# Four token blocks deferred to a last phase that uses Strassen's seven products for both feed-forward matrix products

## The chip, the cores and the metric

The kernel runs on one core of a Trainium2 chip. The metric is the time of one execution on the device in microseconds (us). The core has a matrix engine (TensorE; PE in the profile, with PEld for its weight loads), VectorE (DVE), ScalarE (ACT), GpSimd (POOL) and a queue engine (SyncE, SP) that issues the transfers here. Each engine takes its instructions strictly in program order and waits for the others through semaphores.

## What is computed

Block-causal attention over 8 batches, 8 heads, 576 positions and head width 64, and then a feed-forward network on the 4608 tokens of width 512, with hidden width 2048:

```python
def _attn_ref(q, k, v):                     # (8, 8, 576, 64) each
    scores = scale * np.matmul(q, k.transpose(0, 1, 3, 2))
    scores = np.where(block_i >= block_j, scores, -1000000000.0)   # blocks of 64 positions
    scores = scores - np.max(scores, axis=-1, keepdims=True)
    attn = np.exp(scores)
    attn = attn / (np.sum(attn, axis=-1, keepdims=True) + 1e-09)
    return np.matmul(attn, v)

def _moe_ref(x, w_in, w_out):               # x: (4608, 512), from all heads of a token
    h = x @ w_in                            # (512, 2048)
    g = h * (1.0 / (1.0 + np.exp(-h)))      # silu
    return g @ w_out                        # (2048, 512)
```

## The kernel before

All matrix products are done in a rounded 32-bit form. To keep the precision, each operand is split into a high part (a rounded copy, by ScalarE: `hi`, `x_hi`, `g_hi`, `p_hi`, `split_hi`) and a low part (the rest, by GpSimd: `lo`, `x_lo`, `g_lo`, `p_lo`, `split_lo`). A product is then three matmuls: high by high, high by low, low by high.

**Attention** has 64 units, one for each batch and head (`Unit`). A unit's steps are: `scores` (TensorE, into three banks of the accumulation memory, named S), `max` and `max2` (VectorE), `sub` (VectorE: scores minus maximum into T, which frees the banks), `exp` and `p_hi` (ScalarE), `p_lo` (GpSimd), `sums` (VectorE), `pv` (TensorE, into U), `lower` (ScalarE), `fold` (VectorE, into the feature tile xu), and for each second head `mult` by the reciprocal sums and then `x_hi` and `x_lo`, which put the features of two heads into the ring `xbuf` of 16 tiles. The first positions of each batch are done apart (`First`, `Second`).

**The feed-forward part** has 18 blocks of 256 tokens with 8 steps each. A step is four pieces on TensorE, called "ffn" in the code: twice `ffn1` (12 matmuls of 256 columns each into h) and twice `ffn2` (6 matmuls of 512 columns each into o, two steps later), with `silu` and `g_hi` on ScalarE and `g_lo` on GpSimd between them. A ring tile is free when the last step of its block has read it.

**The order** of all engines' work is the program's order. A written-out list, ORDER, gives it for the weights' preparation and the first 17 units. A loop then takes each further unit i in a fixed order: scores and max of i, fold and mult of i-2, max2 of i, the split of i+1, some pieces (`ffn(pace - 3)`), the features of i-2, sums and pv of i-1, sub of i, lower of i-1, exp, p_hi and p_lo of i, and `ffn(3)`. What is left of the pieces is run behind the loop. The pace is set by one line:

```python
pace = 6 + (count[0] <= AHEAD + 7 * (i - TABLE))
```

## Time and profile before

| What | Value |
|---|---|
| Median of 3 runs | 1041.24 us (1041.07 to 1041.69) |
| Profiled execution, span | 1040.4 us |
| TensorE busy | 1032.7 us, 99% |
| VectorE, ScalarE, GpSimd busy | 762.8, 745.9 and 750.0 us |
| Moved by transfers | 79.95 MB |
| Attention's last score group starts | at 889.45 us |

The time of the profiled execution itself is not recorded apart from its span; the runs' median lies 0.84 us above the span. In the timeline a row has the start, the time to the end of the row's last instruction, the engine, the source line, the output and the input by their names in the program, and how many instructions of the kind follow one another. A duration of a matmul row holds the time until its result has left the array, so the cost of a group on TensorE is the distance to the start of the next group. In brackets is how long the engine was idle before the row, and who ended it.

### The profile page before, as it was taken

The page shows a single profiled execution, that of the slowest core. Times are in us where ns is not written, and L with a number is a line of the kernel's source. Part 1 is how long each engine was busy: PE and PEld are TensorE (multiplying, and loading weights), DVE is VectorE, ACT ScalarE, POOL GpSimd, SP SyncE. Part 2 cuts the span into 40 slices and gives each one's busy share as a digit, 9 for nine tenths or more (in the row PEclk, how much of TensorE's full clock was granted, in tenths as well). Part 3 has the DMA queues.
Part 4 walks back from the last instruction along what each step waited for, and adds up shares of the span by engine and source line. Part 5 has one row for each costly group of instructions (what it writes and reads, how often), then busy time and mean ns, then how long its engine had stood idle before and what let it go on. Part 6 is the DMA issues. An engine that isn't in the chain of part 4 may idle for free.

```text
span 1040.4 us, 20218 instructions
## 1 busy us (share of the span) xinstructions
PE 1032.7 (99%) x7162; PEld 938.7 (90%) x7162; DVE 762.8 (73%) x2233; ACT 745.9 (72%) x1192; POOL 750.0 (72%) x726
## 2 busy tenths in 40 slices
PE   8999999999999999999999999999999999999998
PEld 8888899999999999999999999998999999989987
DVE  7998499999968988888878888888888888700000
ACT  4876498888987888787878787878787777722222
POOL 5775679988997878787878787878787878622221
PEclk9999999999999999999999999999999999999999
DMA  7865232232222222232222222222222222000000
GB/s 264 280 212 198 75 97 74 71 87 67 65 71 74 54 55 74 54 81 59 82 56 75 59 75 54 65 64 54 75 55 74 55 74 55 25 3 21 1 21 21
DMA packets 35188, 79.95 MB, mean 77 GB/s; under 512 B 4752, under 2 KB 13200, under 8 KB 35088
## 3 DMA queue, kind: packets, MB, share of 16 engines
q1 hardware_dynamic: 35088, 78.66, 27.2%
q8 instruction: 57, 0.93, 0.4%
q14 instruction: 43, 0.35, 0.1%
HBM read 69.21 MB, written 9.44 MB: 76 GB/s over the span
## 4 chain that ended last, share of the span: by engine, by line
PE 89%; POOL 4%; DVE 3%; DMA 1%; issue 1%; ACT 1%; SPq 0%; POOLq 0%; DVEq 0%; ACTq 0%
PE h L620 36%; PE o L660 36%; PE S L308 8%; PE U L387 8%; POOL pl L363 1%; DMA qk<-in_qk_dram 1%; PE S L660 1%; DVE wm L235 1%; PE S L578 1%; POOL qh L284 1%; DMA wst<-in_moe_w_out_dram 1%; POOL g L638 1%; DVE S L229 0%; POOL ql L286 0%; DVE S L225 0%
## 5 line engine op out<-in xcount | busy, mean ns | idle before, releaser
L620 PE MATMUL h<-x,wi 128*128 128x256 f32 x3456 | 441.0, 282 | 0.3 <-POOL x L424 0.3
L620 PEld LDWEIGHTS h<-x,wi 128*128 128x128 f32 x3456 | 430.0, 188 | 11.5 <-issue 0.5
L660 PE MATMUL o<-wo,g 128*128 128x512 f32 (+1 forms) x1680 | 423.9, 397 | 0.0
L660 PEld LDWEIGHTS o<-wo,g 128*128 128x128 f32 x1680 | 305.7, 188 | 62.6 <-issue 0.7
L363 POOL TENSOR_TENSOR pl<-p,ph 128x448 fp32r<-128x448 f32 (+1 forms) x192 | 226.0, 1202 | 92.9 <-ACT ph L355 92.9
L638 POOL TENSOR_TENSOR g<-g,g 128x512 fp32r<-128x512 f32 x144 | 186.4, 1294 | 120.3 <-ACT g L633 110.1
L252 DVE TRANSPOSE_TENSOR_REDUCE Mx<-S 64x4 f32<-64x128 f32 (+4 forms) x384 | 135.5, 405 | 92.9 <-PE S L308 92.7
L627 ACT ACTIVATE g<-h 128x512 f32<-128x512 f32 x144 | 86.1, 598 | 124.0 <-POOL g L638 76.3
L633 ACT CAST g<-g 128x512 fp32r<-128x512 f32 x144 | 89.3, 620 | 58.8 <-PE o L660 56.8
L252 DVE TRANSPOSE_TENSOR_REDUCE Dx<-p 128x14 f32<-128x448 f32 (+3 forms) x320 | 122.5, 445 | 0.1
L349 ACT ACTIVATE p<-T 128x512 f32<-128x512 f32 (+1 forms) x192 | 105.2, 604 | 14.8 <-POOL ph L365 13.8
L355 ACT CAST ph<-p 128x512 fp32r<-128x512 f32 (+1 forms) x192 | 104.1, 596 | 1.3 <-PE U L387 1.2
L284 POOL TENSOR_TENSOR qh<-qkraw,qh 64x576 fp32r<-64x576 f32 x64 | 91.8, 1434 | 16.6 <-ACT qh L280 7.7
L672 DVE TENSOR_TENSOR ot<-S,ot 128x256 f32<-128x256 f32 x1 | 0.4, 424 | 125.3 <-PE S L660 125.3
L308 PE MATMUL S<-qh 128*128 128x448 f32 (+3 forms) x320 | 91.1, 298 | 0.0
L627 ACT ACT_TABLE_LOAD x65 | 83.4, 1283 | 1.2
L308 PE MATMUL S<-ql,qh 128*128 128x448 f32 (+3 forms) x320 | 84.0, 307 | 0.0
L349 ACT ACT_TABLE_LOAD x61 | 78.3, 1283 | 1.3 <-DVE Dx L252 0.2
L286 POOL TENSOR_TENSOR ql<-qkraw,qh 128x448 fp32r<-128x448 f32 x64 | 74.1, 1158 | 5.0
L387 PE MATMUL U<-ph,vc 128*128 128x448 f32 (+3 forms) x320 | 74.0, 296 | 0.3 <-POOL vc L295 0.3
L340 DVE TENSOR_TENSOR T<-S,MR 128x256 f32<-128x256 f32 (+2 forms) x192 | 72.8, 405 | 0.0
L280 ACT CAST qh<-qkraw 128x1024 fp32r<-128x1024 f32 x64 | 66.9, 1045 | 7.3 <-DMA qkraw<-in_qk_dram 4.8
(121 smaller groups left out, 1175.3 us busy)
## 6 DMA issues: line engine op xcount, KB each, us to landing
qkraw<-in_qk_dram SPq DMA_DIRECT2D x128, 256.0 KB, 3.9
vraw<-in_v_dram SPq DMA_DIRECT2D x64, 160.0 KB, 2.3
wst<-in_moe_w_out_dram SPq DMA_DIRECT2D x15, 512.0 KB, 5.1
out_dram<-ot SPq DMA_DIRECT2D x23, 256.0 KB, 2.9
wst<-in_moe_w_in_dram SPq DMA_DIRECT2D x10, 512.0 KB, 5.4
out_dram<-ot SPq DMA_DIRECT2D x26, 128.0 KB, 2.4
v<-in_v_dram SPq DMA_DIRECT2D x12, 256.0 KB, 6.1
T<-in_moe_w_in_dram SPq DMA_DIRECT2D x6, 512.0 KB, 4.2
```

Of the source, the lines that this page charges most:

```text
L252: nc.vector.tensor_reduce(out=out, in_=in_, axis=AX.X, op=op, apply_transpose=True)
L284: nc.gpsimd.tensor_tensor(out=u.qh[64:, NQ:], in0=u.raw[64:, NQ:], in1=u.qh[64:, NQ:], op=ALU.subtract)
L308: nc.tensor.matmul(u.ps(c, w, m), u.kk[:, j * P : j * P + m], qq[:, q0 : q0 + w], start=i == 0, stop=i == 1)
L349: nc.scalar.activation(u.p[:, c:e], T[:, c:e], AF.Exp, scale=SCALE)
L355: nc.scalar.copy(u.ph[:, c:e], u.p[:, c:e])
L363: nc.gpsimd.tensor_tensor(out=u.pl[:, c:e], in0=u.p[:, c:e], in1=u.ph[:, c:e], op=ALU.subtract)
L387: nc.tensor.matmul(U[:m, q0 : q0 + w], u.vc[:, j, :m], (u.ph, u.pl)[pp][:, c : c + w], start=n == 0, stop=n == 8)
L620: nc.tensor.matmul(h[:, f, :], wi[wt][:, c, w], x[:, xt, :], start=n == 0, stop=n == 3 * CT - 1)
L627: nc.scalar.activation(g, hs.pop((blk, d)), AF.Silu)
L633: nc.scalar.copy(g2[:, 0], g)
L638: nc.gpsimd.tensor_tensor(out=g2[:, 1], in0=g, in1=g2[:, 0], op=ALU.subtract)
L660: nc.tensor.matmul(o, g2[:, gt, f, tk], wo[wt][:, 2 * d + f, c], start=(d == 0 or i > 0) and n == 0, stop=d == NSTEP - 1 and n == 5,)
```

## The change

Blocks 14 to 17 (`LATER`) leave the usual steps. Their features go from xu to DRAM (`x_dram`, on SP's queue) in place of `x_hi` and `x_lo`. The pace of the loop is now spread evenly over its units, with 16 pieces left behind it (`TAIL`). Where the ring has no free tile for new features, the loop first runs pieces until there is one.

After the loop the attention's memory is released, and a table of events with planned times (`at`) sets the order of a last phase. The four blocks are taken as two double blocks of 512 tokens. The first product is done by Strassen's scheme: for each double block and each of eight slices of 256 hidden columns an `item` has seven products of 6 matmuls with 256 columns. Sums of quarter matrices are made ahead: `prep_x` for features, `prep_s` for the first weights. The products share banks: X takes the products 1, 6, 7 and 4 one after another, and ScalarE copies the sum out between them (`keep`). The results go through silu and to DRAM (`save`). The second product takes one block at a time, again in seven products (`mult_c`), in four groups of 42 matmuls a block; `prep_t` makes its weight sums in place of the first weights, and `prep_g` loads and splits the hidden values.

```diff
+LATER = (14, 15, 16, 17)
+TAIL = 16
+ITEM = 4.94
+FULL = 1.41
...
+                if z[0] in LATER:
+                    dbl, half = divmod(LATER.index(z[0]), 2)
+                    yield None, x_dram[dbl][:, z[1], half * TB + col : half * TB + col + n], src
+                    continue
...
         def x_hi(u):
-            for _, x, src in u.pieces():
-                nc.scalar.copy(x[:, 0, :], src)
+            for z, x, src in u.pieces():
+                if z is None:
+                    nc.sync.dma_start(out=x, in_=src)
+                else:
+                    nc.scalar.copy(x[:, 0, :], src)
...
-        split = t and (blk, d) == (NBLK - 1, NSTEP - 1)
-        if split:
-            outs[blk][t] += [(bank(0)[:, :HD], slice(HD, DM))]
...
-    steps += [(blk, d) for blk in range(2, NBLK) for d in range(NSTEP)]
+    steps += [(blk, d) for blk in range(2, NBLK) if blk not in LATER for d in range(NSTEP)]
...
+    total = 4 * len(steps)
...
-        pace = 6 + (count[0] <= AHEAD + 7 * (i - TABLE))
+        pace = AHEAD + (total - TAIL - AHEAD) * (i + 1 - TABLE) // (n + 2 - TABLE) - count[0]
...
         ffn(pace - 3)
         if z and z.h % 2:
+            while len(x_free) < z.fresh():
+                ffn(1)
             z.x_hi()
             z.x_lo()
...
+    def parts(t, h, l, src, eng, lag=0.9):
+        at(t, lambda: A.copy(h, src()))
+        at(t + lag, lambda: tt(eng, l, src(), h, SUB))
...
+    def prep_t(t, d):
...
+        at(t, lambda: tt(G, z[0], f32(B[0]), f32(B[1]), ADD))
+        ops(t + 2.6, V, q(0), q(1), q(0), SUB)
+        ops(t + 3.0, V, q(1), q(3), q(1), SUB)
+        ops(t + 3.5, V, q(3), q(3), q(0), SUB)
+        ops(t + 3.9, V, q(2), q(2), q(3), SUB)
+        parts(t + 3.5, H[:, 0:2], L[:, 0:2], q(0, 2), V)
+        parts(t + 4.4, H[:, 2:4], L[:, 2:4], q(2, 4), G)
...
+    def item(t, u, d, k):
...
+        p = ITEM / 7
+        for n, (i, o) in enumerate(((1, "X"), (2, "Y"), (6, "X"), (5, "Z"), (7, "X"), (3, "Z"), (4, "X"))):
+            at(t + n * p, prod, i, o)
+        at(t + p + 0.01, keep, A, "s1", "X")
+        at(t + 2 * p + 0.01, add, V, (0, 0), "Y", "s1")
+        at(t + 2.6 * p, silu2, 0)
+        at(t + 3 * p + 0.01, keep, A, "s2", "X")
+        at(t + 4 * p + 0.01, keep, V, "s5", "Z")
+        at(t + 5 * p + 0.01, keep, A, "s3", "X")
+        at(t + 5.6 * p, add, G, (1, 1), "s5", "s3")
+        at(t + 6 * p + 0.01, add, V, (1, 0), "Z", "s2")
+        at(t + 6 * p + 0.45, silu2, 1)
+        at(t + 7 * p + 0.1, save, 1)
+        at(t + 7 * p + 0.15, silu21)
+        at(t + 7 * p + 0.5, save, 0)
...
+    for u in range(nuse):
+        if u == 0 or order[u] != order[u - 1]:
+            prep_x(u * span - 14.0, u)
+        for e in range(HALFD):
+            d = e + HALFD * (u >= NDBL)
+            t = u * span + e * ITEM
+            if u in (0, NDBL):
+                prep_s(t - 6.5 - (u > 0) * 1.5, d)
+            item(t, u, d, u * HALFD + e)
+    for d in range(HALFD):
+        prep_t(end_b - span - 13.0 + 6.0 * d, d)
+        prep_t(end_b - span + 11.0 + 5.5 * d, HALFD + d)
...
+        for q in range(4):
+            k = 4 * n + q
+            t = end_b + k * ITEM
+            prep_g(t - 13.0, blk, q, combs[k % len(combs)], "raw" if k > 5 and k % 2 else "rx")
+            at(t, mult_c, z, q, combs[k % len(combs)])
```

On TensorE, in the 45th attention unit, this stands before: the last score matmuls (S), and then pieces (h, o) ahead of p·v, four with the three behind it making seven.

```order
L308 MATMUL S_8590<-qh 64x64
L308 MATMUL S_8590<-ql,qh 64x64
L620 MATMUL h<-x,wi_73 128x256 x2
L620 MATMUL h<-x,wi_74 128x256
L620 MATMUL h<-x,wi_73 128x256 x2
```

And this stands there now, in the first unit behind the burst of 17 pieces:

```order
L326 MATMUL S_8350<-qh 64x64
L326 MATMUL S_8350<-ql,qh 64x64
L405 MATMUL U<-ph,vc 128x448
L405 MATMUL U<-ph,vc 128x320
L405 MATMUL U<-ph,vc 128x192
L405 MATMUL U<-pl,vc 64x192
```

The pieces between scores and p·v have moved away, most of them into the burst of the unit ahead; p·v now comes right behind the scores, and three pieces follow it.

On ScalarE, in the last stretch of the program, silu (out of h) and the high part of g alternate before:

```order
L627 ACTIVATE g<-h 128x512
L633 CAST g_12842<-g 128x512
L627 ACTIVATE g<-h 128x512
L633 CAST g_12884<-g 128x512
L669 COPY ot<-o 128x512 x2
```

In an item of the first product's second half it has now the copies out of the X bank (s out of S), silu (g), and between them high parts of weight sums (wi, sv) and of features (x):

```order
L1005 COPY s_12255<-S_12235 128x256
L1013 ACTIVATE g_12236<-g_12236 128x256
L1005 COPY s_12281<-S_12235 128x256
L858 CAST wi_78<-raw 128x2x128
L1005 COPY s_12300<-S_12235 128x256
L858 CAST sv_11387<-raw 128x768
L1013 ACTIVATE g_12237<-g_12237 128x512
L858 CAST x<-rx 128x2x256
L1016 ACTIVATE g_12236<-S_12235 128x256
```

ScalarE has nine instructions in an item where a step had two, and three of these are preparation that stands between a copy and the next one that TensorE needs.

## The prediction

> **What bounds the kernel now.** I read the page's first two sections and its chain of waits, then TensorE's and the other engines' timelines in the loop over attention units and in the last 140 us, then the busy times of single stretches, and last the groups of instructions by shape.

> ```profile
> span 1040.4 us, 20218 instructions
> PE 1032.7 (99%) x7162; PEld 938.7 (90%) x7162; DVE 762.8 (73%) x2233; ACT 745.9 (72%) x1192; POOL 750.0 (72%) x726
> PE 89%; POOL 4%; DVE 3%; DMA 1%; issue 1%; ACT 1%; SPq 0%; POOLq 0%; DVEq 0%; ACTq 0%
> ```

> TensorE is the bound: 99% busy and 89% of the chain. So fewer matmul columns shorten the run, as long as TensorE stays fed. The price of a column stands in the timeline of the pure feed-forward stretch near the end:

> ```profile
> 963.94 2.98 PE L620 MATMUL h<-x,wi 128*128 128x256 f32 x24
> 966.76 2.97 PE L660 MATMUL o<-wo,g 128*128 128x512 f32 x12
> 969.57 2.98 PE L620 MATMUL h<-x,wi 128*128 128x256 f32 x24
> ```

> From start to start, 24 matmuls of 256 columns take 2.82 us and 12 of 512 take 2.81 us. A 256-column matmul is 117.4 ns, weight load included, and width does not matter. One step of a block is 5.63 us, that is four pieces ("ffn" calls) of 1.408 us. Now one attention unit in the loop:

> ```profile
> 609.88 0.36 PE L308 MATMUL S<-qh 128*128 128x448 f32 x1
> ...
> 611.28 3.06 PE L620 MATMUL h<-x,wi 128*128 128x256 f32 x24
> 614.18 2.96 PE L660 MATMUL o<-wo,g 128*128 128x512 f32 x12
> 616.97 0.59 PE L387 MATMUL U<-ph,vc 128*128 128x448 f32 x3
> ...
> 618.30 3.02 PE L620 MATMUL h<-x,wi 128*128 128x256 f32 x24
> 621.16 1.56 PE L660 MATMUL o<-wo,g 128*128 128x512 f32 x6
> 622.56 0.37 PE L308 MATMUL S<-qh 128*128 128x448 f32 x1
> ```

> From scores to scores 12.68 us: seven pieces (9.86) and 2.82 us of scores and p·v. The other engines have some room here, but not much:

> ```profile
> core 0: us, PE busy (x) PEld busy (x) DVE busy (x) ACT busy (x) POOL busy (x), PEclk, DMA share, GB/s
> 202.12:223.26 21.14, 21.14 (x136) 19.24 (x135) 20.33 (x66) 17.22 (x30) 18.45 (x19) 1.00 0.23 59
> 223.26:244.43 21.17, 21.17 (x136) 19.28 (x135) 20.59 (x67) 19.07 (x30) 19.20 (x20) 1.00 0.30 74
> 244.43:265.60 21.17, 21.17 (x142) 19.54 (x140) 19.56 (x63) 17.97 (x29) 18.42 (x20) 1.00 0.24 59
> 864.08:889.45 25.37, 25.37 (x172) 23.46 (x170) 20.80 (x65) 19.65 (x32) 19.63 (x19) 1.00 0.14 37
> ```

> Each row is two units. In the three early ones the hand-written order has 5 and 6 pieces to a unit, a unit takes 10.57 us, TensorE is full, and VectorE is busy 19.56 to 20.59 us of 21.2. In the last row there are 7 pieces a unit and VectorE is busy 20.80 of 25.37. So VectorE needs 10.1 to 10.4 us a unit whatever TensorE does, and a unit cannot be much shorter than 10.57.

> **The end phase, TensorE's share.** Four blocks leave the old form: 4 x 8 steps x 5.63 = 180.2 us go. In their place come 32 items (16 for the first product, 16 for the second) of seven products x 6 matmuls x 256 columns: 42 x 117.4 ns = 4.93 us, 157.8 us in all. That is 22.4 us less, and 1040.4 - 22.4 = 1018.0 if TensorE never waits. The split last product of before (6 extra short matmuls) and its final store are replaced by something alike and cost nothing here.

> **The attention loop after the change.** This is the largest term. The loop's 46 units from the 18th to the 63rd had 318 pieces before, 6 or 7 each, and 102 came behind. Now it is 258 and 34, and how they are spread is counted in the order of TensorE's instructions: seven units have 3 pieces, two have 4, twelve have 5, twenty-two have 6, and three have 8, 12 and 17. Blocks 14 to 17 no longer take features, but the earlier blocks' features are still made at 1.75 blocks in eight units while the new pace uses 5.7 x 8 / 32 = 1.43. The ring of 16 feature tiles fills, and the new inner loop then runs pieces until a tile is free; the pace takes these off the units behind. TensorE's own work in a unit is 2.82 + 1.408 n: 7.04 us for 3 pieces, 8.45 for 4, 9.86 for 5. VectorE cannot use a burst to get ahead, since its next work needs the next unit's scores, which stand behind the burst:

> ```profile
> 610.49 0.65 DVE L252 TRANSPOSE_TENSOR_REDUCE Mx<-S 128x14 f32<-128x448 f32 x1 [1.35 <-PE S L308]
> ...
> 620.74 0.27 DVE L333 TENSOR_TENSOR T<-S,MR 64x128 f32<-64x128 f32 x1
> 623.16 0.65 DVE L252 TRANSPOSE_TENSOR_REDUCE Mx<-S 128x14 f32<-128x448 f32 x1 [2.16 <-PE S L308]
> ```

> From the first maximum to the last subtraction, which frees the score banks, it is 10.5 us in an odd head (and less in an even one, which has the row sums behind it); the 2.16 us of waiting behind is all there was to give. A second loop is as long. It runs from p·v over ScalarE and GpSimd to the next p·v:

> ```profile
> 605.44 0.37 PE L387 MATMUL U<-ph,vc 128*128 128x448 f32 x1
> 605.84 0.46 ACT L292 CAST vc<-vraw 128x320 fp32r<-128x320 f32 x1 [1.62 <-PE U L387]
> 606.33 0.52 ACT L392 COPY t<-U 64x448 f32<-64x448 f32 x1
> 606.87 1.28 ACT L349 ACT_TABLE_LOAD   x1
> 608.17 1.62 ACT L349 ACTIVATE p<-T 128x448 f32<-128x448 f32 x3
> 609.69 1.60 ACT L355 CAST ph<-p 128x448 fp32r<-128x448 f32 x3
> 610.32 3.52 POOL L363 TENSOR_TENSOR pl<-p,ph 128x448 fp32r<-128x448 f32 x3 [2.54 <-ACT ph L355]
> 613.92 0.32 POOL L365 TENSOR_TENSOR ph<-p,ph 64x64 fp32r<-64x64 f32 x1
> ```

> The end of one p·v at 605.8 to the last operand of the next at 614.24 is 8.4 us, and with p·v itself (616.97 to 618.30, 1.33) 9.8. In a unit with 3 pieces p·v comes right behind the scores, so TensorE waits there for GpSimd and then for VectorE's subtraction.

> I take 10.57 us for a light unit, the shortest steady period in the trace. Six units of 3 pieces wait 3.53 us each, 21.2. The first unit of the loop has no older unit to fold and I give it 1.6. Two of 4 pieces: 2.12 each, 4.2. The twelve of 5 lose up to 0.71 each; the early rows show 5 beside 6 at no loss, so I take 0.3, 3.6. Sum 30.6. Below: 10.1 us a unit and nothing for the fives, 22.6. Above: 11.0 us, because the loop's order is fixed and not hand-placed, 40.

> **Features through DRAM.** The stores to DRAM come on SP's queue behind the load of a later unit, and the vraw load stands behind them. What they hold is the feature tile, which VectorE's next even fold overwrites:

> ```profile
> 618.38 1.10 SPq L272 DMA_DIRECT2D qkraw<-in_qk_dram  x2
> 625.50 0.58 DVE L398 TENSOR_TENSOR xu<-U,t 64x448 f32<-64x448 f32 x1
> out_dram<-ot SPq DMA_DIRECT2D x26, 128.0 KB, 2.4
> ```

> Issue from 619.5, two stores, the second landed at about 619.5 + 0.55 + 2.4 = 622.5; the fold would come 2.1 us earlier than at 625.50, at 623.4. It is covered by 0.9 us. Without that cover twelve pairs would lose under 1 us each. The casts and subtractions of these features on ScalarE and GpSimd leave the loop, into engines that have room. Loading them again (0.5 MB twice, for each of three uses) falls 14 us ahead of need. I take 0 for all, 6 for the upper end.

> **Hand-offs in the end phase.** In the first product TensorE adds several products into one bank (X), and ScalarE must copy it out between two of them; another product of 0.70 us lies between. The hand-off prices:

> ```profile
> 967.02 0.60 ACT L627 ACTIVATE g<-h 128x512 f32<-128x512 f32 x1 [2.20 <-PE h L620]
> L420 ACT CAST x<-xu 128x256 fp32r<-128x256 f32 x32 | 12.9, 403 | 0.8 <-DVE xu L403 0.8
> L424 POOL TENSOR_TENSOR x<-xu,x 128x256 fp32r<-128x256 f32 x32 | 23.7, 739 | 0.2
> L638 POOL TENSOR_TENSOR g<-g,g 128x512 fp32r<-128x512 f32 x144 | 186.4, 1294 | 120.3 <-ACT g L633 110.1 <-issue 5.8 <-POOL wi L246 0.7
> L471 POOL TENSOR_TENSOR MR<-MR,rr 128x1024 f32<-128x1024 f32 x3 | 5.7, 1900 | 1.0 <-DVE rr L468 1.0
> ```

> ScalarE starts 0.26 us after TensorE's next group does (966.76 to 967.02), and a 256-wide copy is 0.40: 0.66 of 0.70, without the way back to TensorE. The longer loop is from product 7 to the next item's product 6: 0.26, copy 0.40, GpSimd's add 0.74, silu over 512 0.60, silu over 256 0.40, copy 0.40, 2.80 us against four products of 0.70, 2.82. Each further crossing is about 0.1 (ScalarE's first third of the ph cast ends at 610.22, GpSimd starts at 610.32), three of them 0.3. So an item with nothing else on ScalarE loses about 0.3 us, 16 items 4.8. Thirteen of the 16 also have the preparation of sums (copies of 0.4 to 0.9 on ScalarE, 1.3 to 1.9 on GpSimd) in the same strict queues. From the start of the weight sums for the second product, 33 us ahead of it, GpSimd has eight times 1.90 + 1.29, five 1024-wide subtractions, and the rest of the items' own, about 49 us of work in 51. I take 0.7 more for each loaded item: 9. The second product has no such loop; its stationary operands are loaded 13 us ahead, and I take 1. Sum 15; from 0 (if every queue finds its place, as planned in the table of times) to 25.

> **Sum.** 1018.0 + 30.6 + 0 + 15 = 1063.6, and the runs' median, 1041.24, lies 0.8 above this span: 1064.4.

> **The clock.** Every window above has PEclk 1.00, and TensorE's waits before are under 1.1 us, so no row here says what a wait of 3.5 us does. [...]

> **Rivals.**
> 1. *TensorE stays the bound.* The light units cost nothing because the other engines catch up during the bursts. Then 1018.0 + 15 + 0.8 = 1034, faster. For it: the early rows hold 10.57 us with TensorE full. Against: scores and subtraction couple the two engines one unit deep, and 7.04 us is below VectorE's 10.1. It decides where the nine lightest units wait under 0.8 us each, because 1041 leaves 7.4 us for them. Chance 0.06, with 0.02 more for a sum that lands on no change.
> 2. *GpSimd and ScalarE bound the first product.* If the eight items of its second half take 7 us, as with GpSimd's 49 us of work plus its waits for ScalarE, 16 us more than TensorE's and the first half 9: 1064 + 10 to 16, about 1077. For it: the order on GpSimd, where 1.9 us adds stand right ahead of the add that silu waits for. Against: the second product can absorb part. Chance 0.15.
> 3. [...] Chance 0.05.
> 4. *Seven products don't save.* If 256-wide matmuls were held by their weight loads, the end phase would last as before: 1086. The rows at 963.94 and 966.76 exclude it nearly. Chance 0.02.

> The forecast has 0.70; its own range is 1047 (22.6 and 5) to 1083 (40 and 25). A median within 0.2% of before cannot be told from no change here.

> **What would show it.** Right: pieces of 256 columns at 117 ns in the end phase and items of 5.2 to 6.5 us in the first product, 4.9 to 5.0 in the second; in the light units p·v waiting for pl and scores for VectorE's T, score groups 10.3 to 11 us apart, VectorE busy above 92% there and nearly idle in the bursts of 12 and 17. TensorE's busy time down by 20, its idle time up by 40 to 50. Wrong: score groups 8 us apart in the light units, or an end phase at 158 us with the loop as short as 495 us. The prediction fails low if VectorE's work packs tighter than 10.1 us or if the items run at 4.93, and high if one late DMA holds the strict queue of SP.

## The result, and the profile after

| | before | after |
|---|---|---|
| median | 1041.15 us (1040.94 to 1041.69) | 1155.59 us (1154.32 to 1157.75) |
| profiled span | 1040.4 us | 1152.6 us |
| mean granted TensorE clock | 1.000 | 0.967 |

After to before is 1.1098, with a 95% interval of 1.108 to 1.1115. The sign was forecast; 1064 and its range up to 1083 were far too low. The page of the changed kernel begins so (busy times, the row of the granted clock, the chain of waits):

```profile
span 1152.6 us, 21493 instructions
PE 1057.3 (92%) x7348; PEld 966.5 (84%) x7348; DVE 948.2 (82%) x2513; ACT 793.9 (69%) x1294; POOL 829.2 (72%) x751
PEclk9999999999999998999999889999999899788999
PE 45%; DVE 28%; issue 8%; ACT 7%; POOL 7%; DMA 4%; SPq 2%; POOLq 0%; DVEq 0%; ACTq 0%
```

TensorE's share of the chain fell from 89% to 45%, VectorE's rose from 3% to 28%. VectorE is 185 us busier, and TensorE is 25 us busier although its columns were to take 22.4 us less: part of its work runs at a lower clock (0.967 in the mean, against 1.000).

Up to the 18th unit the two differ by 0.4 us (310.85 against 311.21). From there the loss has two places. The attention loop lasts 542.8 us (310.85 to 853.63), which is 49.8 more than TensorE's own work in it (46 x 2.82 + 258 x 1.408 = 493.0). The end phase lasts 243.4 where 180.2 of the old form left: 63.2 more. Together that is 113.0; the spans differ by 112.2.

The end phase in two windows, first and second product (TensorE's busy time and count, clock, transfers):

```profile
core 0: us, PE busy (x), PEclk, DMA share, GB/s
905.98:1040.07 134.09, 99.01 (x673) 0.88 0.27 91
1040.07:1149.40 109.33, 91.15 (x673) 0.92 0.29 83
sum 243.42, PE 190.16; mean PE 95.08
```

The row of the granted clock tells what the lower clock costs: 0.12 of 134.09 us and 0.08 of 109.33 us are together 24.8 us.

Where no preparation runs beside them, items go as forecast. In this stretch of TensorE's timeline an item lasts 949.50 - 944.26 = 5.24 us:

```profile
944.26 0.98 PE L1000 MATMUL S<-x,sv 128*128 128x256 f32 x6
945.08 0.88 PE L1000 MATMUL Z<-x,wi 128*128 128x256 f32 x6
945.79 0.94 PE L1000 MATMUL S<-x,sv 128*128 128x256 f32 x6
946.57 0.94 PE L1000 MATMUL Z<-xown,sv 128*128 128x256 f32 x6
947.34 0.89 PE L1000 MATMUL S<-xown,wi 128*128 128x256 f32 x6
948.06 1.60 PE L1000 MATMUL S<-x,wi 128*128 128x256 f32 x12
949.50 0.94 PE L1000 MATMUL S<-x,sv 128*128 128x256 f32 x6
```

Of the four groups of six matmuls that follow a copy out of their bank, three cost 0.77 to 0.82 us; all other groups cost 0.71 to 0.72. The excess of the three over 0.72 is 0.2 of the 0.3 us that a plain item loses; the other 0.1 is the matmul itself, 120 ns here (0.72 for six) where the prediction had 117.4. The loaded items take up to 13 us. The groups of the end phase by shape show why (count, busy us, mean ns of one):

```profile
L849 DVE TENSOR_TENSOR raw<-raw 128x256 f32<-128x256 f32 x84 | 55.2, 657 | 3.9 <-POOL raw L849 1.9
L849 DVE TENSOR_TENSOR g<-S,s 128x256 f32<-128x256 f32 x18 | 7.6, 423 | 21.4 <-ACT s L1005 8.9 <-PE S L1000 6.8 <-ACT s L1122 3.0
L849 POOL TENSOR_TENSOR raw<-wo,wo 128x1024 f32<-128x1024 f32 x8 | 20.8, 2599 | 0.0
L849 POOL TENSOR_TENSOR g<-s,s 128x256 f32<-128x256 f32 x16 | 14.5, 905 | 30.0 <-ACT s L1005 18.5 <-DVE raw L849 4.8 <-issue 4.6
```

The same operation of 256 columns takes VectorE 423 ns where one operand is in the accumulation memory (S) and 657 on average where both are in the on-chip data memory (raw). One collision in the timeline of all engines:

```profile
1061.37 0.75 PE L1111 MATMUL c<-wi,x 128*128 128x256 f32 x2 [2.86 <-ACT x L858]
1061.40 2.35 POOL L849 TENSOR_TENSOR x<-rx,x 128x1024 fp32r<-128x1024 f32 x1 [2.82 <-ACT x L858]
...
1062.18 1.85 DVE L849 TENSOR_TENSOR sv<-rx,xown 128x256 fp32r<-128x256 f32 x1 [0.68 <-ACT xown L858]
...
1063.80 0.58 PE L1111 MATMUL c<-wi,x 128*128 128x256 f32 x1 [1.68 <-POOL x L849]
```

VectorE's 256 columns start 0.78 us into GpSimd's 1024 and end, after 1.85 us, 0.28 us behind them: they waited inside their own duration, which is why no wait for GpSimd shows in the brackets.

### The profile page after: what moved, and what is told of

Its sections match the earlier page's. It is cut to its first block, busy times and chain, and to the rows that moved or that the text cites. A ratio compares the mean times of both kernels' runs of the same rounds, so it can differ in the third digit from the quotient of the medians.

```text
span 1152.6 us, 21493 instructions
## 1 busy us (share of the span) xinstructions
PE 1057.3 (92%) x7348; PEld 966.5 (84%) x7348; DVE 948.2 (82%) x2513; ACT 793.9 (69%) x1294; POOL 829.2 (72%) x751
## 4 chain that ended last, share of the span: by engine, by line
PE 45%; DVE 28%; issue 8%; ACT 7%; POOL 7%; DMA 4%; SPq 2%; POOLq 0%; DVEq 0%; ACTq 0%
PE h L652 15%; PE o L687 15%; PE U L405 5%; PE S L326 4%; DVE Mx L270 3%; DVE Dx L270 3%; DVE raw L849 3%; PE S L1000 2%; DVE rx L849 2%; DVE m L341 1%; DVE Xm L279 1%; DVE xu L416 1%; ACT p L367 1%; POOL pl L381 1%; DVE MR L274 1%
## 5 line engine op out<-in xcount | busy, mean ns | idle before, releaser
L652 PE MATMUL h<-x,wi 128*128 128x256 f32 x2688 | 349.5, 284 | 0.0
L652 PEld LDWEIGHTS h<-x,wi 128*128 128x128 f32 x2688 | 339.8, 191 | 8.5 <-issue 0.5
L687 PE MATMUL o<-wo,g 128*128 128x512 f32 x1296 | 328.9, 399 | 0.0
L687 PEld LDWEIGHTS o<-wo,g 128*128 128x128 f32 x1296 | 238.5, 190 | 48.6 <-issue 0.7
L670 POOL TENSOR_TENSOR g<-g,g 128x512 fp32r<-128x512 f32 x112 | 145.4, 1298 | 57.9 <-ACT g L665 42.7
L270 DVE TRANSPOSE_TENSOR_REDUCE Mx<-S 64x4 f32<-64x128 f32 (+4 forms) x384 | 132.9, 401 | 57.2 <-PE S L326 57.0
L405 PE MATMUL U<-ph,vc 128*128 128x448 f32 (+3 forms) x320 | 78.8, 312 | 34.4 <-DVE xu L421 22.3
L659 ACT ACTIVATE g<-h 128x512 f32<-128x512 f32 x112 | 67.0, 598 | 47.4 <-POOL g L670 31.6
L405 PEld LDWEIGHTS U<-ph,vc 128*128 128x128 f32 x320 | 59.1, 196 | 44.0 <-POOL ph L383 27.9
L665 ACT CAST g<-g 128x512 fp32r<-128x512 f32 x112 | 69.4, 620 | 22.2 <-PE o L687 20.2
## 6 DMA issues: line engine op xcount, KB each, us to landing
rx<-gd SPq DMA_DIRECT2D x44, 128.0 KB, 2.7
```

What stands on the lines that cost most here:

```text
L270: nc.vector.tensor_reduce(out=out, in_=in_, axis=AX.X, op=op, apply_transpose=True)
L405: nc.tensor.matmul(U[:m, q0 : q0 + w], u.vc[:, j, :m], (u.ph, u.pl)[pp][:, c : c + w], start=n == 0, stop=n == 8)
L652: nc.tensor.matmul(h[:, f, :], wi[wt][:, c, w], x[:, xt, :], start=n == 0, stop=n == 3 * CT - 1)
L659: nc.scalar.activation(g, hs.pop((blk, d)), AF.Silu)
L670: nc.gpsimd.tensor_tensor(out=g2[:, 1], in0=g, in1=g2[:, 0], op=ALU.subtract)
L687: nc.tensor.matmul(o, g2[:, gt, f, tk], wo[wt][:, 2 * d + f, c], start=d == 0 and n == 0, stop=d == NSTEP - 1 and n == 5,)
```

## Experiments on the end phase

Theory A: VectorE's instructions with two operands in the data memory and GpSimd's exclude one another; strict queues then pass the delay on to ScalarE's copies and to TensorE (of its waits in the end phase 19.4 us end with such a copy, L1005). Before the change every VectorE instruction with two operands but one (`p<-p,rr`, L471, 1.72 us) had one of them in the accumulation memory, so next to nothing of this was to be seen.

**p_probe: the disputed cost by itself.** A kernel that computes nothing of the task, run once. Both engines are let go by one gate and run chains of subtractions, alone and together; behind them, groups of 90 matmuls follow waits of several lengths.

```python
open_gate(); vec(16, 256, gate, gate2); vec(8, 512, gate, gate2); close()   # VectorE alone
open_gate(); gps(6, 1024); gps(6, 512); close()                             # GpSimd alone
open_gate(); vec(32, 256, gate, gate2); gps(8, 1024); close()               # both
...
open_gate(); vec(32, 256, ps, gate); gps(8, 1024); close()                  # VectorE: one operand in accumulation memory
```

> This kernel computes nothing of the reference; it runs five stretches of subtractions on VectorE and GpSimd, alone and together, and then groups of 90 matmuls of 256 columns with waits of about 1 to 7 us between them. Theory A (the two engines exclude one another when VectorE reads two operands from the on-chip memory SBUF): VectorE's 256-wide subtraction takes about 0.41 us alone and 1 us or more beside GpSimd's 1024-wide ones, some of them about as long as one GpSimd instruction (1.9 us); with one operand from the accumulation memory it stays at 0.41 us beside the same GpSimd work. Rival B (no exclusion, the long durations come from something else in the end phase): 0.41 us in all three. [...]

Groups of the windows 0 to 30 us, 30 to 60 (rows 3 and 4) and 90 to 120 us:

```profile
L57 POOL TENSOR_TENSOR pv<-gate,gate 128x1024 f32<-128x1024 f32 x4 | 9.4, 2338 | 21.2 <-ACT gate L44 21.0
L53 DVE TENSOR_TENSOR dv<-gate,gate 128x256 f32<-128x256 f32 x16 | 6.8, 425 | 5.2 <-ACT gate L44 4.7
...
L57 POOL TENSOR_TENSOR pv<-gate,gate 128x1024 f32<-128x1024 f32 x8 | 19.1, 2391 | 3.4 <-ACT gate L44 2.8
L53 DVE TENSOR_TENSOR dv<-gate,gate 128x256 f32<-128x256 f32 x6 | 12.7, 2108 | 28.7 <-ACT gate L44 28.6
...
L53 DVE TENSOR_TENSOR dv<-ps,gate 128x256 f32<-128x256 f32 x25 | 10.6, 424 | 4.6 <-ACT ps L45 3.8
```

VectorE goes from 425 to 2108 ns an instruction beside GpSimd, which itself goes from 2338 to 2391 only. The mean of 2108 holds one that ran ahead in 0.43 us; the next eight take 2.44 us each, one for each of GpSimd's eight. With one operand in the accumulation memory VectorE keeps 424. This trace agrees with theory A, with 425 against 2108 ns.

**e_vector: no GpSimd in the end phase.**

```diff
-    V, G, A = nc.vector, nc.gpsimd, nc.scalar
+    V, G, A = nc.vector, nc.vector, nc.scalar
```

> The changed kernel with all of GpSimd's work in the last phase given to VectorE, nothing else. Theory A (exclusion between the two engines): VectorE's instructions fall back to about 0.41 us for 256 and 0.68 us for 512 columns, its work in the last phase sums to about 190 to 200 us, and this is the new bound: the phase takes 195 to 215 us where it took 243, the kernel 1105 to 1130 us. Rival B (the queues are simply overloaded and wait for one another): the same work on one queue fewer is worse, the phase takes 270 us or more, the kernel 1180 us or more.

1113.39 us (1113.11 to 1115.43), 1.0694 [1.0676, 1.0711] of before: 42.2 us come back although VectorE now does GpSimd's work as well, as theory A expected. VectorE's most frequent group, and the sum of busy times over the end phase, first in this kernel (907.16 to 1108) and then in the changed one (905.98 to 1149.40):

```profile
L849 DVE TENSOR_TENSOR raw<-raw 128x256 f32<-128x256 f32 x84 | 35.4, 421 | 1.4
```

```profile
sum 200.84, PE 175.33 PEld 168.82 DVE 167.77 ACT 94.76 POOL 0.00; mean PE 175.33 PEld 168.82 DVE 167.77 ACT 94.76 POOL 0.00
sum 243.42, PE 190.16 PEld 181.62 DVE 177.68 ACT 95.54 POOL 127.43; mean PE 95.08 PEld 90.81 DVE 88.84 ACT 47.77 POOL 63.72
```

VectorE is busy 167.8 us with both engines' work, where it showed 177.7 with its own. But this kernel alone doesn't show how much is exclusion: VectorE is also about twice as fast as GpSimd (1024 columns take 1.22 us against 2.4). The next three tell that.

**e_noprep: no preparations.** `parts` (with ScalarE's copies), `ops` and the other sums of `prep_s`, `prep_t`, `prep_x` and `prep_g` are left out.

```diff
     def parts(t, h, l, src, eng, lag=0.9):
+        return
...
     def ops(t, e, out, a, b, op):
+        return
...
-        at(t, whole, 0)
-        at(t, whole, 1)
...
-        at(t, lambda: tt(G, z[0], f32(B[0]), f32(B[1]), ADD))
```

> The changed kernel without the arithmetic that makes the sums of weights, features and activations and their halves in the end phase (products, evictions, sums of products, SiLU, loads and stores stay; the operands are then whatever lies in the buffers). Theory A (the seven products and their hand-offs cost what plain items show, 5.2 us, and all above it is the preparations): 16 items by 5.2 us = 83 us for the first product and 79 to 84 for the second, instead of 134 and 109: 1155.6 - 51 - 28 = about 1077 us, 1072 to 1084. Rival B (banks, evictions and DMA round trips of the features cost much by themselves): the first product stays over 100 us, 1095 us or more.

1081.94 us (1078.35 to 1083.21), inside A's range. The two products (same columns as for the changed kernel above; the second window begins 1.9 us ahead of the second product):

```profile
core 0: us, PE busy (x), PEclk, DMA share, GB/s
909.80:994.00 84.20, 82.11 (x658) 1.00 0.41 139
994.00:1078.00 84.00, 82.66 (x689) 1.00 0.40 114
sum 168.20, PE 164.76; mean PE 82.38
```

So products, evictions, silu and the round trip of the hidden values through DRAM need 168.2 us, at a granted clock of 1.00. Each item of the second product takes 5.04 us, 42 matmuls of 120 ns. The other 75.2 us of the 243.4 come with the preparations. They split by the two sums: TensorE's idle time grows from 3.4 to 53.3 (49.8 us more), its busy time from 164.8 to 190.2 for the same matmuls (25.4 us of slower clock).

**e_gpsimd and e_vecwork: one engine's preparations at a time.** In the first VectorE's instructions in `parts`, `ops` and `prep_s` are left out, in the second GpSimd's, also the sum in `prep_t`; ScalarE's copies stay in both. Both also keep the raw sums in two fixed tiles, and the first does without one more intermediate tile (tx). The code is of the first.

```diff
-        at(t + lag, lambda: tt(eng, l, src(), h, SUB))
+        if eng is not V:
+            at(t + lag, lambda: tt(eng, l, src(), h, SUB))
...
-        at(t, lambda: tt(e, out(), a(), b(), op))
+        if e is not V:
+            at(t, lambda: tt(e, out(), a(), b(), op))
```

> The changed kernel, with VectorE's share of the end phase's preparations left out (sums and low halves that VectorE makes; so the operands are not the right ones), and all of GpSimd's and ScalarE's kept. With all preparations left out it took 1081.9 us, with all of them 1155.6: 73.7 us. Theory A (the two engines' instructions exclude one another, and most of the 73.7 comes from both being there): GpSimd's work alone, some 100 us in 243, fits beside the products: end phase 170 to 190 us instead of 243, 1085 to 1102 us. Rival B (GpSimd's slow instructions in strict queues cost most by themselves, and the gain of moving them to VectorE came from VectorE being twice as fast): 1115 us or more.

> The mirror of the run before: GpSimd's share of the preparations left out, VectorE's and ScalarE's kept; GpSimd keeps only the 256-wide sum of each item. Theory A: VectorE's 256-wide instructions take 0.41 to 0.43 us instead of 0.66 and the end phase 172 to 185 us: 1085 to 1097 us, and the losses of the two runs over 1081.9 together stay under half of the 73.7. Rival B': VectorE's load alone costs most of it, 1115 or more. If the two losses add to about 73.7, there is no interaction and exclusion is not the cause.

1092.89 us (1091.33 to 1096.35) with GpSimd's alone, 1092.71 (1091.78 to 1094.16) with VectorE's alone. Over the kernel without preparations that is 10.9 and 10.8, ScalarE's copies included in each; both together cost 73.7. So 52 us exist only when both engines work, and rivals B and B' are out. Two groups of GpSimd in the first, VectorE's sums in the second, and the second's busy times over 178 us of the end phase (PE, PEld, DVE, ACT, POOL):

```profile
L856 POOL TENSOR_TENSOR raw<-wo,wo 128x1024 f32<-128x1024 f32 x8 | 19.2, 2395 | 0.1
L856 POOL TENSOR_TENSOR g<-s,s 128x256 f32<-128x256 f32 x16 | 11.8, 738 | 23.8 <-ACT s L1015 23.8
```

```profile
L856 DVE TENSOR_TENSOR raw<-raw 128x256 f32<-128x256 f32 x84 | 40.2, 478 | 1.8
```

```profile
910.00:1088.00 178.00, 167.22 (x1324) 163.80 (x1322) 114.88 (x255) 90.57 (x192) 18.44 (x24) 0.98 0.38 117
```

GpSimd's 905 ns are 738 and its 2599 are 2395. VectorE is 114.9 us busy where the changed kernel, over 243.4 us and with 13 instructions more in the window, has 177.7. From 900 us to the end, where the counts are 272 and 273, it is 123.6 against 183.5: some 60 us of VectorE's time there was blocking. GpSimd's 79 instructions of the phase take 117.0 us in e_gpsimd and 127.4 in the changed kernel, 10 us more. A part of the 52 may also be the chain from VectorE's sums over ScalarE's copies to GpSimd, which each of the two kernels breaks; these runs don't divide that.

## Experiments on the attention loop

In TensorE's timeline of the changed kernel, an odd unit with three pieces:

```profile
649.48 0.22 PE L326 MATMUL S<-ql,qh 128*64 128x64 f32 x1
654.82 1.14 PE L405 MATMUL U<-ph,vc 128*128 128x448 f32 x3 [5.12 <-DVE xu L421]
...
657.41 3.60 PE L652 MATMUL h<-x,wi 128*128 128x256 f32 x24
```

p·v waits 5.12 us for `mult` (L421), which uses the bank of U for the reciprocal sums, and stands in VectorE's strict order behind the row sums and the next maximum. Over the loop this is the largest of TensorE's waits (us in total, times, longest); pl and T, which the prediction named, have 0.7 us each:

```profile
PE U L405 <- DVE xu L421: 22.3, 9, 5.6
PE S L326 <- DVE T L356: 0.7, 1, 0.7
PE U L405 <- POOL pl L381: 0.7, 1, 0.7
```

Behind its 5.12 us p·v takes 2.59 us up to the pieces (1.33 before, 616.97 to 618.30, at a clock of 1.00), and the 24 matmuls behind it 3.43 us (to 660.84) instead of 2.82: the granted clock is 0.50 in the first stretch and 0.81 in the second. VectorE in the unit behind:

```profile
660.51 0.27 DVE L351 TENSOR_TENSOR T<-S,MR 64x128 f32<-64x128 f32 x1
662.44 0.69 DVE L696 COPY ot<-o 128x512 f32<-128x512 f32 x1 [1.66 <-PE o L687]
663.05 2.21 DVE L270 TRANSPOSE_TENSOR_REDUCE Mx<-S 128x14 f32<-128x448 f32 x6
```

and then it waits 1.66 us for TensorE. The two engines wait for each other in turn.

**e_smooth: an even pace instead of bursts.**

```diff
-        pace = AHEAD + (total - TAIL - AHEAD) * (i + 1 - TABLE) // (n + 2 - TABLE) - count[0]
+        k = i + 1 - TABLE
+        pace = AHEAD + (13 * k // 2 if k <= 27 else 175 + (total - TAIL - AHEAD - 175) * (k - 27) // (n + 2 - TABLE - 27)) - count[0]
```

> The changed kernel with 6 and 7 pieces a unit up to the 44th unit, so that the ring never fills and no burst is needed, and 4 or 5 in the units behind it; nothing else. Theory A (what is lost in the attention loop comes from units with 3 and 4 pieces behind bursts, at a floor of 10.6 us a unit): the loop waits 20 to 25 us in place of 49, the kernel takes 1127 to 1132 us, and the last phase is as long as before this edit. Rival B (a light unit's floor is 11.7 us, since p.v also waits for its bank): the 4s and 5s lose 2 us each and the kernel gains 10 us or less, 1145 us or more.

1142.28 us (1141.27 to 1142.59): 13.3 gained, loop waits 36.0. Between the theories, nearer B: the bursts' removal gave only a quarter, because 26 units with 6 or 7 pieces leave 19 with 4 or 5, which lose 1.7 us each.

**e_preload: the table load out of the chain.** In e_smooth ScalarE's load of the exponential's table (1.28 us) stood behind VectorE's subtraction.

```diff
             w.lower()
         if u:
+            nc.scalar.activation(tiny, tiny0, AF.Exp, scale=SCALE)
             for part in (u.exp, u.p_hi, u.p_lo):
```

> The kernel with the even pace of 6 and 7 pieces to unit 43 (1142.3 us, 36.0 us of waits in the attention loop, 1.8 us in each of the units 44 to 62 with four or five pieces), and one exponential of a constant ahead of the real ones, so that ScalarE's table load of 1.28 us does not stand behind VectorE's subtraction. Theory A (the light units are set by the chain maximum, subtraction, table load, exponentials, low halves, p v, and the load has come into that chain): each of the 19 light units loses 1.28 us less, as far as it lost that much: loop waits 12 to 18 us, 1120 to 1126 us. Rival B (the single bank of U, which the multiplication of the pair holds until p v may write it, sets the light units): p v goes on waiting for VectorE's multiplication, under 5 us gained, 1138 us or more. If the added exponential is in the way on ScalarE in the full units, slower than 1142.

1139.32 us (1137.53 to 1140.72), 1.0944 [1.0925, 1.0964] against e_smooth's 1.0963 [1.0946, 1.0979]: not told apart from no gain. The load no longer waits for the subtraction, but p·v waits for VectorE as before, as rival B had it:

```profile
778.24 1.14 PE L405 MATMUL U<-ph,vc 128*128 128x448 f32 x3 [3.83 <-DVE xu L421]
...
780.83 4.13 PE L690 MATMUL o<-wo,g 128*128 128x512 f32 x12
```

The 12 matmuls behind it take 3.96 us (to 784.79) instead of 2.81. VectorE has no gap between 762.6 and 784.2 there. Its pair of units lasts 21.7 us (10.3 and 11.36 in the steady stretch), of which two output copies (`ot`) are 1.2. So a light unit costs 10.83 us of VectorE, and its limit is VectorE, not the table.

**e_both: e_preload and e_vector together.**

> The kernel of the run before and VectorE in place of GpSimd for the end phase's sums and low halves. The two causes lie in different stages, so they should add: the time of the run before less 42 us (the gain that VectorE alone brought, 1155.6 to 1113.4): 1078 to 1085 by theory A, 1095 to 1100 by rival B of the run before. Either way still slower than before the change (1041), since the end phase's loaded items keep waits that VectorE's own load makes.

1101.05 us (1099.61 to 1102.53): 38.3 less than e_preload, where 42.2 were expected, and 1 us above rival B's range. The gains of the two stages add nearly, not wholly.

**e_spread: other blocks put off.**

```diff
-LATER = (14, 15, 16, 17)
-TAIL = 16
+LATER = (10, 14, 16, 17)
+TAIL = 0
```

> The changed kernel with other blocks put off: 10, 14, 16 and 17 in place of 14 to 17, and no pieces held back by the pace (TAIL 0). The work is the same. The ring of feature tiles then never fills, and the attention loop has 3 and 5 pieces in its first two units and 6 in nearly all others, in place of 3 to 17; 19 pieces stand behind it instead of 34. TensorE's own work is 11.27 us in a unit with 6 pieces and VectorE's about 10.8. Theory A (light units are set by VectorE's 10.8 us a unit, and the loss comes from the uneven spread alone): loop waits 5 to 9 us in place of 49.8, 1155.6 - 43 = about 1113 us, 1108 to 1118. Rival B (the stores of features to DRAM and the waits that they put on fold and on the queue of loads cost much by themselves, whatever the pace): more than 25 us of waits in the loop, 1130 us or more.

1126.76 us (1125.67 to 1127.43). The loop came out as theory A has it: 8.5 us of waits, 6 pieces and 11.3 us a unit. A window of it:

```profile
410.00:510.00 100.00, 100.00 (x651) 91.83 (x650) 91.83 (x289) 84.99 (x130) 83.99 (x82) 1.00 0.28 74
```

TensorE is full at clock 1.00, and the stores of features are all still there: rival B is out. Yet 28.8 us came back, not 43. The time lies outside both theories' ranges (1108 to 1118, and 1130 or more). The rest went at the start of the end phase, where 19 pieces instead of 34 cover the first preparations; TensorE's first items:

```profile
872.66 2.38 PE L1000 MATMUL S<-x,wi 128*128 128x256 f32 x7 [6.45 <-ACT x L858]
...
888.06 1.65 PE L1000 MATMUL S<-xown,sv 128*128 128x256 f32 x6 [11.31 <-ACT s L1005]
```

17.8 us of waits in two rows; the changed kernel has 5.5 there. I had not priced that cover.

**e_spreadv: e_spread without GpSimd in the end phase.**

> The kernel of the run before (blocks 10, 14, 16, 17 put off, even pace), with VectorE in place of GpSimd for the end phase's sums and low halves. The two stages are apart, so the gains add: 42 us less than the run before, about 1071 us (1066 to 1078). Even so slower than before the change (1041): the end phase still has some 40 us of waits, from VectorE's 168 busy us in about 200, and the saving in matmul columns is 22.4. If it came under 1050, the two causes would hold each other up and were counted too low.

1089.03 us (1086.25 to 1091.37), 37.7 less than e_spread, 1.0452 [1.0428, 1.0477] of before. The expected 1066 to 1078 was missed: it started from e_spread at 1113, and the gain is again 4 us under 42. The fastest version here is still 48 us slower than the kernel before; none was found that beats it.

## Why the prediction was right or wrong

- **Columns, -22.4: right within 3.5 us.** A matmul of the end phase costs 120 ns, not 117.4, so the 1344 of them take 161.3 us where the sum had 157.8. A plain item takes 5.2 us as forecast, and without preparations both products take 168.2, where the sum had 157.8 + 15.
- **Hand-offs in the end phase, 15 (0 to 25): the step that failed.** By the forecast's own sum the term came out at 85.6 (243.4 - 157.8). The plain items' 0.3 was right. The 0.7 for each loaded item and the 1 for the second product, 10 in all, should have been about 75 (243.4 - 168.2). The working counted the preparations of ScalarE and GpSimd, each by its own load; VectorE's sums and low halves had no term. That VectorE's preparations and GpSimd's block each other was not in it: 52 of the 73.7 us that the preparations cost come only with both. GpSimd's sums of 1024 columns were also priced too low, at 1.90 us from a row with another input; alone they take 2.40. The new instructions' operands could be read from the diff (`raw` out of `raw`), and no row of before covered them; such a term needed a wide range, not one that ends at 25.
- **Attention loop, 30.6 (22.6 to 40): right engine, wrong wait, too small.** Measured 49.8. VectorE sets the light units, as forecast. But p·v does not wait for the low halves there, nor the scores for T: p·v waits for `mult`, which holds U's bank (22.3 us). Six of the seven units of 3 pieces come in pairs of some 9.3 and 14 us and not at 10.3 to 11. Seven units of 3 pieces lose 29.4 (forecast 22.8), two of 4 4.5 (4.2), twelve of 5 11.6 (3.6), the rest 4.3 (0). The floor of 10.57 left out the output copies and the mutual waits: two units of 3 pieces last 23.3 to 23.9 us. TensorE's idle time in the loop is 35.9 us (542.78 - 506.93 busy), inside the range; some 10 us of the rest is lower clock, by the difference to e_spread and by the granted clock of 0.98 over the 542.78 us.
- **Features through DRAM, 0: held.** With all stores in place e_spread's loop has 8.5 us of waits in all, and in the changed kernel the fold waits for a store 1.2 us in sum.
- **Rival 2 (GpSimd and ScalarE bound the first product, 1077)** had the place, not the cause: GpSimd's and ScalarE's load without VectorE's costs 10.9 us.
- **Rival 3 (the clock)**: a lower clock was to be added to the forecast rather than set against it. The sum put the clock at full speed throughout, the 1.00 of every window before; the mean granted clock came out at 0.967. Most of the loss by it fell in the end phase, 25.4 us.
- **Rivals 1 and 4** are out: the light units wait, and the columns are saved.

## What to carry to other kernels

When a change moves elementwise work onto two engines at once, look at where each operand lies and at what runs beside it: loads that fit each engine alone cost 11 us each here and 74 together. An engine that waits inside an instruction shows as busy (VectorE's most frequent sum took 657 ns on average here and 421 in e_vector), so compare mean durations of equal shapes before believing a busy share. Deferred work should be chosen so that the loop left behind stays evenly filled (choosing other blocks took its waits from 49.8 to 8.5 us), and enough of it must stay to cover the next phase's start.

## What the runs showed of the hardware

```profile
142.25 11.05 PE L83 MATMUL o<-xs,w 128*128 128x256 f32 x90 [0.78 <-DVE w L88]
155.59 12.54 PE L83 MATMUL o<-xs,w 128*128 128x256 f32 x90 [2.29 <-DVE w L88]
171.09 13.62 PE L83 MATMUL o<-xs,w 128*128 128x256 f32 x90 [2.96 <-DVE w L88]
224.61 12.62 PE L83 MATMUL o<-xs,w 128*128 128x256 f32 x90 [5.14 <-DVE w L88]
```

Behind a wait of 0.78 us the group takes 11.05 us; behind waits of 2.29 us and more it takes 1.5 to 2.6 longer, and a longer wait adds no more (the longest, 6.59 us, adds 2.1). The mean granted clock of that run is 0.880. No run kept TensorE's clock up in the changed kernel with all else equal, so the 25.4 us are read from its busy times and its granted clock, not tested apart.
